# adaLN block with local dilated attention and GEGLU: first products interleaved over two PSUM banks, first norm scaled chunk by chunk, 14 warm-up products, another written-out order

## The chip, the core and the metric

The kernel runs on one core of one Trainium2 chip. The metric is device time in microseconds (us) of one execution; the median of several runs is compared. A profile is taken of one execution more, and all lines of a trace in this document come from such a profile.

## The reference

One transformer block on x of 2048 rows by 512 columns (bf16), with shift, scale and gate vectors (sa, ca, ga, sb, cb, gb) from `silu(c) @ w_mod`.

```
h   = layernorm(x) * (1 + ca) + sa
qkv = h @ wqkv                      # 32 heads of 16
logits[s, w] = q[s] . k[s - 2w] / 4   for w = 0..7, masked where s - 2w < 0
o   = sum_w softmax(logits)[s, w] * v[s - 2w]
x   = x + ga * (o @ wo)
h   = layernorm(x) * (1 + cb) + sb
x   = x + gb * ((gelu(h @ w_gate) * (h @ w_up)) @ w_down)   # inner width 1792
```

## The kernel before

**Tiling.** The 2048 rows are four groups of 512 rows (`sg` 0 to 3); a group is four chunks of 128 rows (`c4`). The 512 columns are four pieces of 128 (`dt`), the inner width 1792 is 14 pieces (`ft`).

**Stages of a group**, with the names that the profile and this text use:

- First norm `LN1.sg`. VectorE (DVE) takes mean and variance of a chunk (`st`, lines 410 and 411, 0.8 us a chunk), or ScalarE (ACT) does it for the chunks that the table `ACT_CH` names (`sa` line 388, `nm` line 394, `sq` line 399). DVE adds epsilon (`vd` line 436 for its own chunks, `va` line 441 for ACT's), GpSimd (POOL) raises to -1/2 (`rs`, line 447), and DVE scales the chunks (`x`, line 424).
- Transposes on TensorE (PE), or by DMA for some groups; then scale and shift by the modulation vectors give the pieces `h0` to `h3` of hT (ACT line 498; in group 0 ACT line 516 and DVE line 514, half a group at a time).
- Products `qp.sg.blk.j`: 12 for a group, each 4 matmuls over `dt` into one PSUM bank (line 565; in group 0 the first two are done in halves of 256 rows, `qph`, line 547). ACT copies each out (lines 579, 581, 585).
- Logits: DVE multiplies q by shifted k (`pq`, line 631, 2.3 us, four a group), PE sums over the head (`lp`, line 645), DVE and ACT do the softmax, DVE multiplies by v (`pv`), PE sums (`o`, line 796), or in group 3 DVE does (`os` line 758, `ot2` line 763, `ob` line 770).
- Output projection `x1p` (line 817), added to x by DVE (`x1`, line 826); second norm `LN2.sg`; products `g` and `u` (line 845), ACT's gelu `gl` (line 878) and copy `ub` (line 885), DVE's product `hh` (line 896); then `y` (line 857, in the last chunk line 868), DVE's sum `ot` (line 903), and the store.

**PSUM.** The pool `mm` has 4 banks, shared by qkv, g, u, y, the vectors of modulation (`mp`) and the warm-up products. The buffers of `gl` and `ub` are three each: a fourth `gl` waits for `hh` of the third before it.

**Order.** Nothing is scheduled at run time. Each stage of each group is a generator ("thread") of `Op`s; the list `ORDER` says which thread issues its next op. It fixes the sequence on each engine's queue, DMA issues on SP and ACT included. The numbers in an `Op` (its cost, `lat`) are not used when the kernel is built; `after` is only asserted.

**At the start**, PE runs 20 products on a zeroed tile (`warmup`, line 213, spread between the first real ones), then `mp1`, `mp0` (line 296: columns of the modulation vectors, from `wm1`, `wm0`), the transposes `th0`, `th1` of group 0's two halves (line 483), and `qph`. The op `pre` (line 330) is a four-element Exp on ACT, ahead of which the exp table is loaded. POOL builds small constants (`consts`, `M2`).

Sequences of the queues where the text needs them (from `ORDER`, thread by thread):

```
PE, start        8 warm, scp, 8 warm, mp1, 2 warm, mp0, th0, th1, 2 warm, qph ...
PE, group 1      LN1.1.t0, mp2, t1, mp3, lp.0.0-2, lp.0, qp.1.0.0, qp.1.1.0, qp.1.2.0-3, LN1.2.t0 ...
ACT, start       s4, scT, pre, scB, mod1, mod0, h0.0, h1.0, h0.1, LN1.1.sa3 ...
DVE, start       st0, st1, vd0, st2, st3, vd2, x0, x1, x2, x3, h2.0, h3.0, h1.1, h2.1, h3.1, LN1.1.st0 ...
DVE, group 3     ... pv.3.3, hh.2.0, hh.2.1, os.3.1, ot2, ob, os.3.2, ot2, ot.1.1, ot.1.2, ob, os.3.3, ot2, ob, hh.2.2, hh.2.3, ot.1.3 ...
SP               ... x2, wo0, wo1, wm2, wm3, wo2, wo3, x3, vst.0, gst2, wm4, V4.0.0 ...
```

Of the kernel before, what the change touches and what calls it, by code (L numbers as in the profile page):

```python
# [8 lines left out]
ACT = mybir.ActivationFunctionType  # L9
ALU = mybir.AluOpType  # L10
AX = mybir.AxisListType
F32 = mybir.dt.float32
# [93 lines left out]
def kernel(  # L106
# [13 lines left out]
    nc = tc.nc  # L120
    P = 128
# [95 lines left out]
    def loads():  # L217
# [43 lines left out]
        def act_q():  # L261
            yield Op("ACT", 0.45, ldc, fire="c", lat=0.0, dma=True)
            yield Op("ACT", 0.46, ldx(0, 2, 4, nc.scalar), fire="x0.2", lat=1.45, dma=True)

        def sp_q():
            yield Op("SP", 0.47, ldx(0, 0, 2), fire="x0.0", lat=1.0)
            yield Op("SP", 0.47, ldwm(1), take=[SL["h2"]], fire="wm1", lat=3.2)
            yield Op("SP", 0.5, ldwm(0), take=[SL["h2"]], fire="wm0", lat=1.4)
            yield Op("SP", 0.55, ldq(0), fire="wqkv0", lat=mb(0.5))
            yield Op("SP", 0.55, ldx(1), fire="x1", lat=mb(0.5))  # L270
            yield Op("SP", 0.55, ldq(1), fire="wqkv1", lat=mb(0.5))
            yield Op("SP", 0.55, ldq(2), fire="wqkv2", lat=mb(0.5))
            yield Op("SP", 0.55, ldx(2), fire="x2", lat=mb(0.5))
            for i in range(4):
                yield Op("SP", 0.45, ld(woP[H * i:H * i + H, :, :], wo_v[i]), fire=f"wo{i}", lat=0.42)
            yield Op("SP", 0.55, ldx(3), fire="x3", lat=mb(0.5))
# [97 lines left out]
    ACT_CH = {"LN1.1": (3, 4), "LN1.2": (2, 4), "LN1.3": (0, 4), "LN2.0": (0, 2), "LN2.1": (0, 4), "LN2.2": (0, 2), "LN2.3": (0, 2)}  # L374
# [28 lines left out]
    def norm(key, src, ready, ev, parts=((0, 4),)):  # L403
        aa, ab = ACT_CH.get(ev, (0, 0))
        dv = [c4 for c4 in range(CPS) if not aa <= c4 < ab]
        for c4 in dv:
            def f(c4=c4):
                k = norm_tiles(ev)
                st = stat.tile([P, 6], F32, name="st")
                nc.vector.bn_stats(out=st[:], in_=src()[:, c4, :])  # L410
                nc.vector.bn_aggr(out=k["mv"][:, c4, :], in_=st[:])
            yield Op("DVE", 0.815, f, after=ready(c4), fire=f"{ev}.st{c4}")
            for a, b in parts[:-1]:
                if c4 == b - 1:
                    yield from rst(ev, a, b, [c4 for c4 in dv if a <= c4 < b])
        a, b = parts[-1]
        yield from rst(ev, a, b, [c4 for c4 in dv if a <= c4 < b])
        for c4 in range(CPS):
            def f(c4=c4):
                k = norm_tiles(ev)  # L420
                if c4 == 0:
# [4 lines left out]
            yield Op("DVE", 0.325, f, after=[f"{ev}.rs{max(a for a, b in parts if a <= c4)}"],  # L426
                     take=[SL["xn"]] if c4 == 0 else [], fire=f"{ev}.x{c4}")
# [112 lines left out]
    def qkv_halves():  # L540
        for half in range(2):
            def f(half=half):
                for j in range(2):
                    if half == 0:
                        B["qkvps", 0, 0, j] = T("mm", [P, SG], F32, "qkv_ps")
                    for dt in range(DT):
                        nc.tensor.matmul(B["qkvps", 0, 0, j][:, half * 256:half * 256 + 256],
                                         lhsT=wqkv[0][:, dt, j::4], rhs=B["hT", 0][:, 2 * half:2 * half + 2, dt, :],
                                         start=(dt == 0), stop=(dt == DT - 1))
            yield Op("PE", 0.87, f, after=[f"LN1.0.h{d}.{half}" for d in range(DT)] + ["wqkv0"],  # L550
                     take=[SL["mm"]] * 2 + [SL["q"]] if half == 0 else [], fire=f"qph.{half}")
        for j in range(2):
            pl.done[f"qp.0.0.{j}"] = pl.done["qph.1"]

    def qkv(sg):
        if sg == 0:
            yield from qkv_halves()
        for n, (blk, j) in enumerate(QKV if sg else QKV0):
            if (sg, blk) == (0, 0) and j < 2:
                continue  # L560
# [192 lines left out]
    def osum(sg):  # L753
        for i in range(4):
# [4 lines left out]
            yield Op("DVE", 2.19, f, after=[f"pv.{sg}.{i}"], take=[SL["prod"]], give=[SL["prod"]], fire=f"os.{sg}.{i}")  # L759
# [4 lines left out]
            yield Op("DVE", 1.12, f, fire=f"ot2.{sg}.{i}")  # L764
# [72 lines left out]
    def ffn_mm(sg):  # L837
        h2 = [f"LN2.{sg}.h3"]
        for ft in range(FT):
# [95 lines left out]
    pl.spawn(warmup(13, 20))  # L935
# [3 lines left out]
    for sg in range(NSG):  # L939
        for n, g in (("sa1", lambda q: norm_act(lambda: B["x", q], lambda c4: [f"x{q}"], f"LN1.{q}")),  # L940
# [37 lines left out]
```

## Time and profile before

| what | value |
|---|---|
| median of 3 runs | 238.0 us (237.67 to 238.57) |
| the profiled execution | 237.54 us |
| its span, first to last instruction | 235.8 us |
| busy share: PE, DVE, ACT, POOL | 97%, 77%, 66%, 5% |
| granted TensorE clock, mean | 1.000 |
| chain that ended last, by engine | PE 75%, DVE 14%, ACT 8% |
| PE LDWEIGHTS busy | 108.9 us (46%) |
| DMA, mean | 121 GB/s |

The span is the time between the first and the last instruction; 1.74 us of the profiled execution lie outside. "Busy" of PE counts matmuls from start to modelled end, and since they are pipelined (a 128x512 product has a row of 379 ns, while neighbours start 216 ns apart), PE is read here from starts, not from busy time.

### The profile page before, as it was taken

Reading aid. Unit: us, or ns where it says so; the run is one execution under the profiler, and the core shown is the slowest. Engines: PE = TensorE matmul, PEld = TensorE weight load, DVE = VectorE, ACT = ScalarE, POOL = GpSimd, SP = SyncE. Lnnn points to the kernel's source line nnn. Section 1 sums busy time; section 2 is a strip of 40 time slices with the busy share of each in tenths; the row PEclk is TensorE's granted clock in tenths of the full one; section 3 lists DMA queues with packets and bytes.
Section 4 is the critical chain, followed back from the end, with each engine's and each line's share of the span. In section 5 each row is a group of like instructions: output and inputs, shape, how many; then the busy total and the mean of one; then the engine's idle time right before and its main releaser. Section 6 shows DMA issues by size and latency. Waiting matters only on the chain.

```text
span 235.8 us, 3655 instructions
## 1 busy us (share of the span) xinstructions
PE 229.8 (97%) x1371; PEld 108.9 (46%) x1371; DVE 182.2 (77%) x244; ACT 154.7 (66%) x301; POOL 12.5 (5%) x37
## 2 busy tenths in 40 slices
PE   7999899999999999999999999999999999999995
PEld 2656364544544444444444444444344444444444
DVE  3889999999999999999999899999728521222222
ACT  4589999986996649957687878422567343667400
POOL 1620101000100000100000100000000100000000
PEclk9999999999999999999999999999999999999999
DMA  6998797999965859634104014001230141000011
GB/s 216 350 306 233 219 196 176 192 347 326 195 172 162 288 120 198 155 70 120 59 0 100 1 37 98 25 0 67 62 95 3 31 102 44 3 0 0 0 44 44
DMA packets 36792, 28.64 MB, mean 121 GB/s; under 512 B 15784, under 2 KB 35368, under 8 KB 36776
## 3 DMA queue, kind: packets, MB, share of 16 engines
q1 hardware_dynamic: 36496, 28.17, 46.4%
q10 hardware_dynamic: 280, 0.26, 0.3%
q8 instruction: 10, 0.16, 0.3%
q14 instruction: 6, 0.05, 0.1%
HBM read 21.08 MB, written 5.24 MB: 112 GB/s over the span
## 4 chain that ended last, share of the span: by engine, by line
PE 75%; DVE 14%; ACT 8%; issue 1%; DVEq 0%; ACTq 0%
PE u_ps L845 16%; PE g_ps L845 15%; PE y_ps L857 14%; PE qkv_ps L565 12%; PE x_ps L817 6%; DVE os L758 4%; DVE pv L738 4%; PE warm_ps L213 3%; PE o_ps L796 2%; PE LTp L645 2%; DVE hht L896 2%; ACT vT L585 2%; ACT gl L399 2%; DVE os L763 2%; ACT gl L388 2%
## 5 line engine op out<-in xcount | busy, mean ns | idle before, releaser
L845 PE MATMUL u_ps<-h,Wu 128*128 128x512 bf16 x224 | 57.5, 379 | 0.5 <-ACT gl L878 0.5
L845 PE MATMUL g_ps<-h,Wg 128*128 128x512 bf16 x224 | 57.5, 379 | 0.0
L878 ACT ACTIVATE gl<-g_ps 128x512 bf16<-128x512 f32 x56 | 33.6, 600 | 20.6 <-PE g_ps L845 16.7
L857 PE MATMUL y_ps<-Wd,hht 128*128 128x512 bf16 x210 | 46.3, 379 | 0.0
L885 ACT CAST ub<-u_ps 128x512 bf16<-128x512 f32 x56 | 32.9, 587 | 20.3 <-PE u_ps L845 20.2
L565 PE MATMUL qkv_ps<-hT,wqkv 128*128 128x512 bf16 x184 | 41.8, 380 | 0.6 <-ACT qT L579 0.6
L896 DVE TENSOR_TENSOR hht<-gl,ub 128x512 bf16<-128x512 bf16 x56 | 22.1, 418 | 23.5 <-ACT ub L885 23.4
L631 DVE TENSOR_TENSOR pq<-qT,kT 128x4096 bf16<-128x4096 bf16 x16 | 36.0, 2284 | 0.7 <-ACT kT L581 0.7
L845 PEld LDWEIGHTS <-Wu 128*128 128x128 bf16 x224 | 21.6, 98 | 27.9 <-issue 2.5
L845 PEld LDWEIGHTS <-Wg 128*128 128x128 bf16 x224 | 21.8, 98 | 26.8 <-issue 0.8
L857 PEld LDWEIGHTS <-hht 128*128 128x128 bf16 x210 | 20.6, 98 | 24.8
L565 PEld LDWEIGHTS <-wqkv 128*128 128x128 bf16 x184 | 20.3, 114 | 20.3 <-issue 3.3
L748 DVE TENSOR_TENSOR pv<-PT,V 128x4096 bf16<-128x4096 bf16 x12 | 26.7, 2282 | 0.0
L903 DVE TENSOR_TENSOR ot<-y_ps,x 128x512 bf16<-128x512 f32 x15 | 10.1, 686 | 14.7 <-PE y_ps L857 14.7
L447 POOL TENSOR_TENSOR rstd<-rstd,neghalf 128x4 f32<-128x4 f32 (+1 forms) x9 | 8.6, 961 | 170.7 <-DVE rstd L441 164.8
L498 ACT ACTIVATE h<-h,modT,scl 128x512 bf16<-128x512 bf16 x12 | 8.8, 802 | 9.7 <-DMA h<-xn 9.7
L817 PE MATMUL x_ps<-woP,oT 128*128 128x512 bf16 x64 | 15.1, 379 | 0.0
L826 DVE TENSOR_TENSOR x<-x_ps,x 128x512 bf16<-128x512 f32 x16 | 10.7, 682 | 3.1 <-PE x_ps L817 3.0
L410 DVE BATCH_NORM_STATS2 st<-x 128x6 f32<-128x512 bf16 x15 | 10.1, 676 | 3.0 <-DMA x<-in_A_x_dram 3.0
L399 ACT ACTIVATE gl<-x,sums 128x512 bf16<-128x512 bf16 x17 | 12.3, 730 | 0.2
L388 ACT ACTIVATE gl<-x 128x512 bf16<-128x512 bf16 x17 | 10.7, 643 | 2.2 <-DVE x L826 2.0
L581 ACT CAST kT<-qkv_ps 128x512 bf16<-128x512 f32 x16 | 9.8, 612 | 0.9 <-PE qkv_ps L565 0.8
(82 smaller groups left out, 202.5 us busy)
## 6 DMA issues: line engine op xcount, KB each, us to landing
V<-vscr SPq DMA_DIRECT2D x8, 520.0 KB, 11.3
wm<-in_w_mod_dram SPq DMA_DIRECT2D x6, 512.0 KB, 4.7
vscr<-vT SPq DMA_DIRECT2D x4, 512.0 KB, 4.9
out_dram<-ot SPq DMA_DIRECT2D x15, 128.0 KB, 1.8
Wg<-in_B_w_gate_dram SPq DMA_DIRECT2D x1, 1792.0 KB, 9.1
Wu<-in_B_w_up_dram SPq DMA_DIRECT2D x1, 1792.0 KB, 12.7
wqkv<-in_A_wqkv_dram SPq DMA_DIRECT2D x3, 512.0 KB, 7.7
x<-in_A_x_dram SPq DMA_DIRECT2D x3, 512.0 KB, 8.5
```

What stands on the lines that cost most here:

```text
L388: nc.scalar.activation(out=gpool.tile([P, D], BF16, name="gl")[:], in_=src()[:, c4, :], func=ACT.Copy, accum_out=k["s"][:, 0, c4:c4 + 1])
L399: nc.scalar.activation(out=gpool.tile([P, D], BF16, name="gl")[:], in_=src()[:, c4, :], func=ACT.Square, bias=k["s"][:, 1, c4:c4 + 1], acc ...
L565: nc.tensor.matmul(ps[:], lhsT=wqkv[blk][:, dt, j::4], rhs=B["hT", sg][:, :, dt, :], start=(dt == 0), stop=(dt == DT - 1))
L631: nc.vector.tensor_tensor(out=pq[:], in0=_ap(B["qT", sg][:, j, :], [[0, W], [1, SG]]), in1=_ap(kT[:, j, sg * SG + 2:sg * SG + 2 + SG], [[2 ...
L748: nc.vector.tensor_tensor(out=t[:], in0=_ap(B["PT", sg][:, 0, :], [[SG, 2], [0, 4], [1, SG]]), in1=_ap(v[:, 0, j, :], [[8, 2], [4 * (SG + ...
L817: nc.tensor.matmul(ps[:], lhsT=B["oT", sg][:, j, c4 * P:(c4 + 1) * P], rhs=woP[:, j, :], start=(j == 0), stop=(j == 3))
L826: nc.vector.tensor_tensor(out=x[:, c4, :], in0=B["x1ps", sg, c4][:], in1=x[:, c4, :], op=ALU.add)
L845: nc.tensor.matmul(ps[:], lhsT=Wt[:, dt, ft * P:(ft + 1) * P], rhs=B["h2T", sg][:, :, dt, :], start=(dt == 0), stop=(dt == DT - 1))
L857: nc.tensor.matmul(ps[:], lhsT=B["hh", sg, ft][:, c4 * P:(c4 + 1) * P], rhs=B["Wd", ft // 4][:, ft % 4, :], start=(ft == 0), stop=(ft == F ...
L878: nc.scalar.activation(out=gl[:], in_=B["g", sg, ft][:], func=ACT.Gelu_apprx_tanh)
L885: nc.scalar.copy(out=ub[:], in_=B["u", sg, ft][:])
L896: nc.vector.tensor_tensor(out=hh[:], in0=B["gl", sg, ft][:], in1=B["ub", sg, ft][:], op=ALU.mult)
```

## The change

1. `warmup(12, 14)`: 14 warm-up products in place of 20.
2. `ACT_CH` gets `LN1.0: (3, 4)`: statistics of chunk 3 of the very first norm go from DVE to ACT; DVE gets one small `va2` for it. The DVE part of `norm` is rewritten: chunks of a part are scaled as soon as the statistics of the next part are issued, so `x0`, `x1` stand ahead of `vd2`. Only `LN1.0` has two parts; for all other norms the sequence is the same.
3. `qkv_halves`: the two products of a half of group 0 go piece by piece over two banks (`qph.half.n`, pieces 2, 0, 3, 1, then 1, 0, 2, 3) where each product ran its four pieces before.
4. `qkv_pair` (new): in groups 1 to 3 the products (q, j=0) and (k, j=0) go piece by piece over two banks (`qpp.sg.dt`). `ffn_mm`: the first `g` and first `u` likewise (`gu.sg.dt`).
5. `ORDER` is another list. The number of matmuls other than warm-up products is the same.

```diff
-    ACT_CH = {"LN1.1": (3, 4), ...
+    ACT_CH = {"LN1.0": (3, 4), "LN1.1": (3, 4), ...
...
+        done = []
+        for a, b in parts:
+            for c4 in dv:
+                if a <= c4 < b:
+                    yield stats(c4)
+            for c4 in done:
+                yield scaled(c4)
+            yield from rst(ev, a, b, [c4 for c4 in dv if a <= c4 < b])
+            done = range(a, b)
+        for c4 in done:
+            yield scaled(c4)
...
     def qkv_halves():
-        for half in range(2):
-            def f(half=half):
-                for j in range(2):
...
+        for half, order in ((0, (2, 0, 3, 1)), (1, (1, 0, 2, 3))):
+            for n, dt in enumerate(order):
+                def f(half=half, n=n, dt=dt):
+                    for j in range(2):
...
+    def qkv_pair(sg):
+        for dt in range(DT):
+            def f(dt=dt):
+                for blk in range(2):
+                    if dt == 0:
+                        B["qkvps", sg, blk, 0] = T("mm", [P, SG], F32, "qkv_ps")
+                    nc.tensor.matmul(B["qkvps", sg, blk, 0][:], lhsT=wqkv[blk][:, dt, 0::4], rhs=B["hT", sg][:, :, dt, :],
+                                     start=(dt == 0), stop=(dt == DT - 1))
...
     def ffn_mm(sg):
-        for ft in range(FT):
+        for dt in range(DT):
+            def f(dt=dt):
+                for nm, Wt in (("g", Wg), ("u", Wu)):
+                    if dt == 0:
+                        B[nm, sg, 0] = T("mm", [P, SG], F32, nm + "_ps")
+                    nc.tensor.matmul(B[nm, sg, 0][:], lhsT=Wt[:, dt, 0:P], rhs=B["h2T", sg][:, :, dt, :],
+                                     start=(dt == 0), stop=(dt == DT - 1))
...
+        for ft in range(1, FT):
...
-    pl.spawn(warmup(13, 20))
+    pl.spawn(warmup(12, 14))
```

What `ORDER` makes of the queues, at the places named above:

```
PE, start        8 warm, scp, 6 warm, th0, mp1, mp0, th1, qph ...
PE, group 1      LN1.1.t0, t1, lp.0.0, lp.0.1, mp2, qpp.1.0-3, lp.0.2, lp.0, mp3, qp.1.2.0-3, qp.1.0.1, qp.1.1.1, qp.1.0.2, LN1.2.t0 ...
PE, group 0 att. ... o.0.0, qpp.3.0, qpp.3.1, o.0.1, lp.1.2, o.0.2, qpp.3.2, qpp.3.3, qp.2.0.2, o.0.3, qp.2.1.2, x1p.0.0, x1p.0.1, lp.1 ...
ACT, start       s4, scT, LN1.0.sa3, nm, sq3, pre, mod1, mod0, h0.0, h1.0, h0.1, LN1.1.sa3 ... (scB later)
DVE, start       st0, st1, vd0, st2, x0, x1, vd2, va2, x2, x3, h2.0, h3.0, h1.1, h2.1, h3.1, LN1.1.st0 ...
DVE, group 3     ... pv.3.3, os.3.1, ot2, ob, ot.1.1, hh.2.0, hh.2.1, ot.1.2, os.3.2, ot.1.3, ot2, ob, os.3.3, hh.2.2, ot2, hh.2.3, ob, hh.2.4 ...
SP               ... x2, wo0, wo1, wo2, wo3, x3, wm2, wm3, vst.0, wm4, gst2, V4.0.0 ...
POOL             ident, consts, LN1.0.rs0, rs2, M2 ... (before: ident, rs0, rs2, consts, M2)
```

In group 2 the output projection `x1p.2.2` stands ahead of `u.1.6` (before: behind it), and `x1p.3.0` behind `u.2.11`.

More of the change, by code (lines that the diff above doesn't have):

```diff
@@ L262, in act_q @@
             yield Op("ACT", 0.45, ldc, fire="c", lat=0.0, dma=True)
-            yield Op("ACT", 0.46, ldx(0, 2, 4, nc.scalar), fire="x0.2", lat=1.45, dma=True)
+            yield Op("ACT", 0.46, ldx(0, 2, 4, nc.scalar), fire="x0.2", lat=2.3, dma=True)
         def sp_q():
             yield Op("SP", 0.47, ldx(0, 0, 2), fire="x0.0", lat=1.0)
-            yield Op("SP", 0.47, ldwm(1), take=[SL["h2"]], fire="wm1", lat=3.2)
+            yield Op("SP", 0.47, ldwm(1), take=[SL["h2"]], fire="wm1", lat=2.45)
             yield Op("SP", 0.5, ldwm(0), take=[SL["h2"]], fire="wm0", lat=1.4)
@@ L372, in woscale @@
         yield Op("DVE", 1.14, wos, after=["ga"] + [f"wo{i}" for i in range(4)], fire="woS")
-    ACT_CH = {"LN1.1": (3, 4), "LN1.2": (2, 4), "LN1.3": (0, 4), "LN2.0": (0, 2), "LN2.1": (0, 4), "LN2.2": (0, 2), "LN2.3": (0, 2)}
+    ACT_CH = {"LN1.0": (3, 4), "LN1.1": (3, 4), "LN1.2": (2, 4), "LN1.3": (0, 4), "LN2.0": (0, 2), "LN2.1": (0, 4), "LN2.2": (0, 2), "LN2.3": (0, 2)}
     NS = {}
@@ L405, in norm, with stats, f @@
         dv = [c4 for c4 in range(CPS) if not aa <= c4 < ab]
-        for c4 in dv:
-            def f(c4=c4):
+        def stats(c4):
+            def f():
                 k = norm_tiles(ev)
@@ L411, in f, with scaled @@
                 nc.vector.bn_aggr(out=k["mv"][:, c4, :], in_=st[:])
[L412 to L419, printed above, removed]
+            return Op("DVE", 0.815, f, after=ready(c4), fire=f"{ev}.st{c4}")
+        def scaled(c4):
+            def f():
                 k = norm_tiles(ev)
@@ L425, in f @@
                                         scalar2=k["rstd"][:, c4:c4 + 1], op0=o, op1=ALU.mult)
-            yield Op("DVE", 0.325, f, after=[f"{ev}.rs{max(a for a, b in parts if a <= c4)}"],
-                     take=[SL["xn"]] if c4 == 0 else [], fire=f"{ev}.x{c4}")
+            return Op("DVE", 0.325, f, after=[f"{ev}.rs{max(a for a, b in parts if a <= c4)}"],
+                      take=[SL["xn"]] if c4 == 0 else [], fire=f"{ev}.x{c4}")
+        done = []
[9 more added lines that the diff above has]
+            yield scaled(c4)
     def rst(ev, a, b, dv):
@@ L540, in qkv_halves @@
     def qkv_halves():
-        for half in range(2):
-            def f(half=half):
-                for j in range(2):
-                    if half == 0:
-                        B["qkvps", 0, 0, j] = T("mm", [P, SG], F32, "qkv_ps")
-                    for dt in range(DT):
+        for half, order in ((0, (2, 0, 3, 1)), (1, (1, 0, 2, 3))):
+            for n, dt in enumerate(order):
+                def f(half=half, n=n, dt=dt):
+                    for j in range(2):
+                        if half == 0 and n == 0:
+                            B["qkvps", 0, 0, j] = T("mm", [P, SG], F32, "qkv_ps")
                         nc.tensor.matmul(B["qkvps", 0, 0, j][:, half * 256:half * 256 + 256],
                                          lhsT=wqkv[0][:, dt, j::4], rhs=B["hT", 0][:, 2 * half:2 * half + 2, dt, :],
-                                         start=(dt == 0), stop=(dt == DT - 1))
-            yield Op("PE", 0.87, f, after=[f"LN1.0.h{d}.{half}" for d in range(DT)] + ["wqkv0"],
-                     take=[SL["mm"]] * 2 + [SL["q"]] if half == 0 else [], fire=f"qph.{half}")
+                                         start=(n == 0), stop=(n == DT - 1))
+                yield Op("PE", 0.2175, f, after=[f"LN1.0.h{dt}.{half}", "wqkv0"],
+                         take=[SL["mm"]] * 2 + [SL["q"]] if half == n == 0 else [], fire=f"qph.{half}.{n}")
         for j in range(2):
-            pl.done[f"qp.0.0.{j}"] = pl.done["qph.1"]
+            pl.done[f"qp.0.0.{j}"] = pl.done["qph.1.3"]
+    def qkv_pair(sg):
[6 more added lines that the diff above has]
+                                     start=(dt == 0), stop=(dt == DT - 1))
+            yield Op("PE", 0.437, f, after=[f"LN1.{sg}.h{dt}", "wqkv0", "wqkv1"],
+                     take=[SL["mm"]] * 2 + [SL["q"]] if dt == 0 else [], fire=f"qpp.{sg}.{dt}")
+        for blk in range(2):
+            pl.done[f"qp.{sg}.{blk}.0"] = pl.done[f"qpp.{sg}.3"]
     def qkv(sg):
@@ L557, in qkv @@
             yield from qkv_halves()
+        else:
+            yield from qkv_pair(sg)
         for n, (blk, j) in enumerate(QKV if sg else QKV0):
-            if (sg, blk) == (0, 0) and j < 2:
+            if (sg == 0 and blk == 0 and j < 2) or (sg and n < 2):
                 continue
@@ L758, in f @@
                 nc.vector.tensor_tensor(out=t[:], in0=a[:, :, 0:4, :], in1=a[:, :, 4:8, :], op=ALU.add)
-            yield Op("DVE", 2.19, f, after=[f"pv.{sg}.{i}"], take=[SL["prod"]], give=[SL["prod"]], fire=f"os.{sg}.{i}")
+            yield Op("DVE", 2.31, f, after=[f"pv.{sg}.{i}"], take=[SL["prod"]], give=[SL["prod"]], fire=f"os.{sg}.{i}")
             def f(i=i):
@@ L763, in f @@
                 nc.vector.tensor_tensor(out=t[:, :, 0:2, :], in0=t[:, :, 0:2, :], in1=t[:, :, 2:4, :], op=ALU.add)
-            yield Op("DVE", 1.12, f, fire=f"ot2.{sg}.{i}")
+            yield Op("DVE", 1.25, f, fire=f"ot2.{sg}.{i}")
             def f(i=i):
@@ L838, in ffn_mm @@
         h2 = [f"LN2.{sg}.h3"]
-        for ft in range(FT):
+        for dt in range(DT):
[5 more added lines that the diff above has]
+                                     start=(dt == 0), stop=(dt == DT - 1))
+            yield Op("PE", 0.437, f, after=[f"LN2.{sg}.h{dt}", "Wg", "Wu"], take=[SL["mm"]] * 2 if dt == 0 else [],
+                     fire=f"gu.{sg}.{dt}")
+        for nm in "gu":
+            pl.done[f"{nm}.{sg}.0"] = pl.done[f"gu.{sg}.3"]
+        for ft in range(1, FT):
             for nm, Wt, wk in (("g", Wg, "Wg"), ("u", Wu, "Wu")):
@@ L939 @@
     for sg in range(NSG):
-        for n, g in (("sa1", lambda q: norm_act(lambda: B["x", q], lambda c4: [f"x{q}"], f"LN1.{q}")),
+        for n, g in (("sa1", lambda q: norm_act(lambda: B["x", q], lambda c4: [f"x{q}"] if q else [f"x0.{c4 // 2 * 2}"], f"LN1.{q}")),
                      ("sa2", lambda q: norm_act(lambda: B["x", q], lambda c4: [f"x1.{q}.{c4}"], f"LN2.{q}")), ("ln1", ln1), ("t1", lambda q: transp(("xn1", q), ("hT", q), "hT", f"LN1.{q}") if q else transp0(("xn1", 0), "LN1.0")), ("h1", lambda q: ln1_ev(q) if q else ln1_ev0(False)), ("qkv", qkv),
```

67 rows, old and new, of the table ORDER are left out of this document.

## The prediction

> **What bounds the kernel now.** First the table of busy time by stretch (columns: stretch, its length, then busy us and instructions of PE, PE's weight loads, DVE, ACT, POOL).
>
> ```profile
> 14.90:54.40 39.50, 38.10 (x317) 19.75 (x315) 39.29 (x39) 35.99 (x78) 2.40 (x3) 1.00 0.91 232
> 54.40:132.00 77.60, 77.60 (x483) 35.10 (x482) 76.33 (x87) 59.49 (x115) 2.05 (x2) 1.00 0.60 144
> 132.00:167.00 35.00, 35.00 (x164) 15.88 (x163) 34.53 (x42) 17.85 (x31) 1.05 (x1) 1.00 0.15 38
> ```
>
> Two engines are full at once up to 167 us: PE, and DVE with 39.29 of 39.50, 76.33 of 77.60 and 34.53 of 35.00 us. After 167 DVE is free (22.58 of 68.80 us) and PE alone sets the end. Then PE's own row in order of time, which names each stall in brackets:
>
> ```profile
> 25.10 0.61 PE L645 MATMUL LTp<-pq,Mph 128*32 128x512 bf16 x8 [0.77 <-DVE pq L631]
> ...
> 29.74 1.89 PE L565 MATMUL qkv_ps<-hT,wqkv 128*128 128x512 bf16 x8 [0.45 <-ACT qT L579]
> ...
> 35.70 2.75 PE L565 MATMUL qkv_ps<-hT,wqkv 128*128 128x512 bf16 x12 [0.18 <-ACT qT L579]
> ...
> 168.00 1.02 PE L845 MATMUL u_ps<-h,Wu 128*128 128x512 bf16 x4 [0.52 <-ACT gl L878]
> ```
>
> By starts (neighbours 0.216 us apart) these stalls are 1.09, 0.61, 0.34 and 0.68 us: three before 36 us, one at 168, nothing between. The chain of waits says what stands behind the last:
>
> ```profile
> 130.36 1.74 PE x_ps L817 x8
> 132.12 0.69 DVE x L826
> ...
> 166.84 0.43 DVE hht L896
> 167.31 0.04 issue
> 167.35 0.60 ACT gl L878
> 167.96 0.04 issue
> 168.00 1.02 PE u_ps L845 x4
> ```
>
> From 132 to 167 the chain runs on DVE: `hh.2.2` at 166.84 comes behind group 3's sums, a gelu waits for its buffer, PE for the gelu's bank. So DVE decides how far PE may run ahead until 167, and PE's stalls decide afterwards.
>
> **The start.** These rows set it (start, duration):
>
> ```profile
> 5.18 1.28 ACT L330 ACT_TABLE_LOAD   x1
> ...
> 7.87 0.73 DVE L424 TENSOR_SCALAR xn<-x,mv,rstd 128x512 bf16<-128x512 bf16 x2
> ...
> 8.87 0.73 DVE L424 TENSOR_SCALAR xn<-x,mv,rstd 128x512 bf16<-128x512 bf16 x2 [0.27 <-POOL rstd L447]
> ...
> 14.86 2.29 DVE L631 TENSOR_TENSOR pq<-qT,kT 128x4096 bf16<-128x4096 bf16 x1 [0.75 <-ACT kT L581]
> ```
>
> DVE. Chunk 2's statistics start at 6.05, when x lands, and end at 6.96. Then `x0`, `x1` run 7.00 to 7.73, 0.87 earlier. The second half is not earlier. ACT begins chunk 3 at 6.05 too; the same five instructions of LN1.1 take from 10.88 to 12.68, 1.80 us, so they end at 7.86. `va2` follows at 7.92, POOL 0.30 later for 0.80 us (its row at 8.04), so `x2`, `x3` run 9.05 to 9.78; they ended at 9.60. Loss 0.18.
>
> ACT. `pre` with its table load now follows `sq3`: 7.87 to 9.38, then `mod1`, `mod0` to 9.55, and the pieces `h` from 9.70, against 9.52. [...]
>
> PE. 14 warm-up products end near 7.4, `th0` runs at 7.8, `mp1` and `mp0` (0.4 each) until 9.05, `th1` waits for `x3` and ends at 10.25. `qph` needs `h2.0` (DVE 9.70 to 10.11) and begins at 10.30 instead of 10.49. Its pieces take 0.22 and the eight `h` arrive every 0.32 on DVE and 0.46 on ACT, in just the order in which they are used; the last, `h3.1`, is there at 11.55, its piece starts at 11.83. End 12.05 against 12.24. The six products taken out (2 by 0.43, 4 by 0.22, 1.7 us) thus bring 0.2: behind them the norm is late.
>
> And that 0.2 goes no further: DVE's full stretch begins with `pq.0.0`, which waits for ACT's copy of k, and ACT, 0.18 late, reaches that at 14.19 (before 14.17). `pq.0.0` at 14.87 instead of 14.86: nothing.
>
> **14.9 to 54 us.** DVE's ops up to `pq.1.3` are the same set, without a gap; so `pq.1.3` still ends at 54.34. PE may now stall less: `qpp.1` begins when `h0` is there. I add ACT's rows: it reaches `LN1.1.h0` at 21.3 instead of 22.80 (`sq3` and the gate copy, 0.86, go behind; PE's products come 0.2 to 0.3 earlier there and an idle 0.28 ahead of 16.76 is used), so `qpp.1` runs about 22.8 to 24.6 where `qp.1.0.0` began at 25.64. On PE's queue `mp2` stands ahead of it and needs `wm2`, which SP now issues behind wo2, wo3, x3. Up to wm2's end the queue has then carried the same bytes as before up to wo3's, and wo3 landed at 23.09: some 0.6 us of waiting, at most. By the sums PE stands 0.5 to 1.1 us ahead at 41 us. It then meets DVE: `o.0.3` needs `pv.0.3` (ends 51.00) and `lp.1` needs `pq.1.3`: 54.40 instead of 54.63. **Kept: 0.23.** The two extra splits between four-column and full products (0.2 us each by the starts at 47.37 to 47.68 and 48.78 to 49.09) lie ahead of this wait and cost nothing.
>
> **54 to 167.** PE had no stall and has the same products, with as many splits: the lead stays 0.23. I checked the waits that the new order makes: `lp.2.1` (pq.2.1 ends 70.03, PE there at 70.27), `gu.0` to `gu.3` (a piece takes 0.43, ACT delivers every 0.67 to 0.71, but between two and six other ops stand ahead of them; the closest, gu.1, begins 0.8 us behind its `h0` and may lack 0.05 at the last piece). `x1p.2.2` moved ahead of `u.1.6` ends DVE's gaps at 131.26 and 132.12 (0.44 and 0.17).
>
> **167.** `hh.2.2` is moved ahead of `ot2` and `ob` (1.26 and 0.61) and behind one `ot` more (0.60): 1.27 earlier, with the gaps up to 1.9. Also `ot.1.3`, which held a fourth bank, is done 7 us earlier. **The stall of 0.68 goes.** Next late is `hh.2.4`, no earlier than before (done at 168.5) and needed 0.5 us after that.
>
> **After 167.** PE's work is the same. LN2.3's four scalings follow each other without two `hh` between (0.67 earlier), and `gu.3.0` comes 3.0 us earlier behind y.2's sixth half: x1p.3.3 to `h0` took 11.5 us, less 0.67, against 11.66 in the new order. No stall, 0.8 us of cover.
>
> **Banks alternating.** 24 products of `qpp`, 32 of `gu` and 16 of `qph` change bank at each product. Before, g and u change it at every fourth, with the same 0.216 us between starts: I take nothing. The dearest change in the rows, into or out of four-column products, costs 0.1; 72 by 0.1 is 7.2 us, the far end. [...]
>
> **Sum.** 0.23 + 0.68 = 0.9 us: span 234.9, the profiled execution 237.54 - 0.9 = 236.6. The median of the runs was 238.0, 0.46 above it, and I forecast on that scale: **237.1**. More than 0.5% (1.2 us, about what a measurement of this kernel tells from no change) would need an earlier `pq.0.0`.
>
> **Rivals.**
>
> - **The clock opens late (slower).** Warm-up products started every 0.427 us until 7.0 and every 0.216 from then, so full speed came 6.0 us after the first product. The new ones end at 7.4; `th0`, `mp`, `th1` fill only half of the time to 10.3. Were the array slow then until 6.0 us of products have run again, PE would lose 3.0 us, of which ACT's lateness hides 0.3: 237.1 + 2.7 = 239.8. It decides from the point where `qph` starts 0.2 us apart instead of 0.11. For it: six fillers stood exactly there. Against: 1.1 idle us at 24 did not lower the clock. Chance 0.15. [...]
> - **`wm2` lands late.** Past 23.2 us `mp2` holds `qpp.1`, ACT's copy, `LN1.3.sq3` and with it `va0` on DVE (needed at 35.2); each us later costs one. At 24.6: 238.5. Chance 0.12.
> - **The table load stops ACT's queue longer than its row**, at most by its own length once more: `h` and `pq.0.0` 1.28 later, 238.4. Against it: 0.02 and 0.01 us beside the row. Chance 0.05.
> - **Alternating banks cost** something: from 237.1 up to 244.3. Chance 0.03.
> - **More comes through at the start** (ACT's copy of k at 13.9, as PE allows): 0.3 more, 236.8 or lower. Chance 0.1.
> - The forecast: 0.55, 236.6 to 237.7 by the runs' own scatter.
>
> The range 236.4 to 239.0 leaves out the late clock's upper part and the dear banks. Below 236.8 lie the last rival and a quarter of the forecast: faster 0.22; above 239.2 the late clock mostly: slower 0.16; within 0.5%: 0.62.
>
> **What would show it.** Right: `xn` pairs near 7.0 and 9.05, `qph` near 10.3 with 0.11 between starts, `pq.0.0` at 14.9, `lp.1` at 54.4, no PE wait for `gl` near 167, 216 ns between products of `qpp` and `gu`. Wrong: starts of 0.2 us in `qph`, PE or ACT waiting at `mp2`, a new gap on DVE before 54 us, which moves the end by its own length.

## The result and the profile after

The changed kernel is a little **slower**: a median of 239.2 us (237.59 to 240.6, 17 runs) against 238.0 us (237.56 to 239.22, 17 runs) for the kernel before, measured side by side. The ratio is 1.005, with a 95% interval of 1.0027 to 1.0073. The forecast was 237.1, "slower" had a chance of 0.16.

The profiled execution took 240.6 us, its span 238.6, with a mean granted clock of 0.986. It is one of the two slowest of the 17, and the runs differ in just that: 5 of 17 have a clock of 1.000 (span 235.6 to 237.2, median 236.0), 10 have 0.993 (237.1 to 238.2, median 237.5), 2 have 0.986 (238.6). The kernel before is at 0.998 or more in 95 of the 99 runs that the experiments below added. So the first line to read is the clock in slices, on the page of the changed kernel (each digit is a fortieth of the span, 6 us):

```profile
PEclk9779999999999999999999999999999999999999
```

Slices two and three, 6 to 18 us, are not at full speed. In the kernel before all forty are a 9. (The slow start itself does not show in the digits: before, the warm-up products came 0.427 us apart until 7.0, in slices that print 9.) PE's row in order of time (start, duration, then what ran; in brackets the idle time and who ended it) shows where. First two rows of the kernel before, then the changed kernel:

```profile
9.03 1.19 PE L483 MATMUL hTp<-ident,xn 128*128 128x128 bf16 x16
...
10.49 1.91 PE L547 MATMUL qkv_ps<-hT,wqkv 128*128 128x256 bf16 x16
```

```profile
4.89 1.59 PE L214 MATMUL warm_ps<-gB 128*128 128x512 bf16 x6
8.50 1.25 PE L492 MATMUL hTp<-ident,xn 128*128 128x128 bf16 x8 [2.02 <-DVE xn L421]
9.54 1.04 PE L297 MATMUL modT_ps<-scT,wm 128*128 128x1 bf16 x32
10.51 1.25 PE L492 MATMUL hTp<-ident,xn 128*128 128x128 bf16 x8
11.55 3.62 PE L556 MATMUL qkv_ps<-hT,wqkv 128*128 128x256 bf16 x16
14.97 1.25 PE L589 MATMUL qkv_ps<-hT,wqkv 128*128 128x512 bf16 x4
```

The warm-up products end at 6.5, then PE rests for 2.0 us. The transposes behind the rest start 0.107 us apart (in the kernel before 0.056), and the 16 products of `qph` take 3.4 us by their starts, 0.213 apart (forecast 0.11). Full speed had come at 5.2 us, when warm-up products went from 0.427 to 0.216 us apart; it was gone at 8.6 and came back at 15.4 (granted clock 1.00 for 3.4 us, then 0.50 for 6.8). The first `pq` starts at 17.81 instead of 14.86: 2.95 us are lost ahead of it.

Not all of the 2.95 us is the clock. DVE's row of chunk 2's statistics says when the second half of x landed, at 7.23 here and at 6.05 in the kernel before; and the run f1 (below), where it landed at 7.19 and the clock stayed at full speed, starts its first `pq` at 15.87. The rows, of the changed kernel and of f1:

```profile
7.23 0.69 DVE L411 BATCH_NORM_STATS2 st<-x 128x6 f32<-128x512 bf16 x1 [1.66 <-DMA x<-in_A_x_dram]
```

```profile
15.87 2.29 DVE L656 TENSOR_TENSOR pq<-qT,kT 128x4096 bf16<-128x4096 bf16 x1 [0.77 <-ACT kT L606]
```

By f1 some 1.0 us of the 2.95 belongs to x, and 1.9 to the clock.

The next loss is in the chain of waits, here from 99.86 us on (start, duration, what). Before, the chain from 94 to 112 us ran on PE alone:

```profile
99.86 1.80 DVE Wd L367 x3
...
102.83 2.33 POOL rstd L456
...
105.19 1.40 DVE xn L421 x4
...
106.64 4.39 DMA h<-xn
...
111.77 2.22 ACT h L507 x3
```

POOL's `rstd` of `LN2.1`, four elements a partition, takes 2.3 us where it took 1.04 before:

```profile
98.26 1.04 POOL L447 TENSOR_TENSOR rstd<-rstd,neghalf 128x4 f32<-128x4 f32 x1 [36.17 <-DVE rstd L441]
```

DVE waits 0.90 us for it, the transposes by DMA and ACT's pieces of h come later, and PE, which begins `gu.1` when its first piece is there, stalls:

```profile
111.99 0.38 PE L868 MATMUL g_ps<-h,Wg 128*128 128x512 bf16 x1
112.21 0.38 PE L868 MATMUL u_ps<-h,Wu 128*128 128x512 bf16 x1
112.62 0.38 PE L868 MATMUL g_ps<-h,Wg 128*128 128x512 bf16 x1
...
113.33 0.38 PE L868 MATMUL g_ps<-h,Wg 128*128 128x512 bf16 x1
...
114.03 0.38 PE L868 MATMUL g_ps<-h,Wg 128*128 128x512 bf16 x1
```

The pairs start 0.63, 0.71 and 0.70 apart; without a stall it is 0.43. The sum of what is too much is 0.75 us.

The rest went nearly as forecast. `lp.1` starts at 57.40, 2.77 later than before, so PE gained 0.18 on DVE's late start (forecast 0.23). The stall of 0.68 near 167 is gone. Alternating g and u start 0.216 apart wherever their piece is there. The account of the two profiled spans, with clock and x in the first term: 2.95 - 0.18 + 0.75 - 0.68 = 2.84, and 238.6 - 235.8 = 2.8.

### The profile page after: what moved, and what is told of

The parts are those of the page before. It is cut to its first block, busy times and chain, and to the rows that moved or that the text cites. A ratio compares the mean times of both kernels' runs of the same rounds, so it can differ in the third digit from the quotient of the medians.

```text
span 238.6 us, 3636 instructions
## 1 busy us (share of the span) xinstructions
PE 230.9 (97%) x1355; PEld 108.9 (46%) x1365; DVE 181.1 (76%) x243; ACT 156.4 (66%) x306; POOL 13.6 (6%) x37
## 4 chain that ended last, share of the span: by engine, by line
PE 68%; DVE 11%; DMA 7%; ACT 7%; issue 3%; POOL 1%; SPq 0%; ACTq 0%; POOLq 0%
PE g_ps L880 16%; PE u_ps L880 16%; PE y_ps L892 15%; PE qkv_ps L589 7%; PE x_ps L841 4%; DMA V<-vscr 3%; DVE pv L772 3%; DMA x<-in_A_x_dram 2%; DVE pq L655 2%; DMA h<-xn 2%; ACT vT L609 2%; PE LTp L669 2%; DVE Wd L367 2%; PE o_ps L820 1%; ACT gl L389 1%
## 5 line engine op out<-in xcount | busy, mean ns | idle before, releaser
L880 PE MATMUL g_ps<-h,Wg 128*128 128x512 bf16 x208 | 53.4, 379 | 0.0
L880 PE MATMUL u_ps<-h,Wu 128*128 128x512 bf16 x208 | 53.4, 379 | 0.0
L589 PE MATMUL qkv_ps<-hT,wqkv 128*128 128x512 bf16 x160 | 36.8, 381 | 0.3 <-ACT qT L603 0.3
L880 PEld LDWEIGHTS <-Wu 128*128 128x128 bf16 x208 | 20.1, 98 | 25.1 <-issue 1.3
L880 PEld LDWEIGHTS <-Wg 128*128 128x128 bf16 x208 | 20.1, 98 | 25.1 <-issue 1.3
L589 PEld LDWEIGHTS <-wqkv 128*128 128x128 bf16 x160 | 17.8, 114 | 16.3 <-issue 1.5
L456 POOL TENSOR_TENSOR rstd<-rstd,neghalf 128x4 f32<-128x4 f32 (+1 forms) x9 | 9.8, 1093 | 173.9 <-DVE rstd L450 170.8
L389 ACT ACTIVATE gl<-x 128x512 bf16<-128x512 bf16 x18 | 11.3, 636 | 6.8 <-DVE x L850 3.7
L400 ACT ACTIVATE gl<-x,sums 128x512 bf16<-128x512 bf16 x18 | 13.1, 738 | 0.2
L603 ACT CAST qT<-qkv_ps 128x512 bf16<-128x512 f32 x16 | 9.7, 612 | 2.6 <-PE qkv_ps L589 1.4
```

Source lines behind the costliest of these rows:

```text
L389: nc.scalar.activation(out=gpool.tile([P, D], BF16, name="gl")[:], in_=src()[:, c4, :], func=ACT.Copy, accum_out=k["s"][:, 0, c4:c4 + 1])
L400: nc.scalar.activation(out=gpool.tile([P, D], BF16, name="gl")[:], in_=src()[:, c4, :], func=ACT.Square, bias=k["s"][:, 1, c4:c4 + 1], acc ...
L589: nc.tensor.matmul(ps[:], lhsT=wqkv[blk][:, dt, j::4], rhs=B["hT", sg][:, :, dt, :], start=(dt == 0), stop=(dt == DT - 1))
L880: nc.tensor.matmul(ps[:], lhsT=Wt[:, dt, ft * P:(ft + 1) * P], rhs=B["h2T", sg][:, :, dt, :], start=(dt == 0), stop=(dt == DT - 1))
```

## The experiments

All were timed beside the kernel before, whose median was 237.8 to 237.9. "Closed" below counts the runs with a granted clock of 0.993 or less. Two theories stood at the start. **Theory:** with fewer warm-up products, and PE at rest for 2.0 us behind them, the clock closes, and `gu.1`'s stall takes away the forecast gain. **Rival:** the clock is beside the point; the norm part or the late arrival of x makes the loss.

| kernel | warm-up products | runs, closed | median us | median span at full clock |
|---|---|---|---|---|
| before (beside all the others) | 20 | 99, 4 | 237.8 to 237.9 | 235.9 to 236.1 |
| changed | 14 | 17, 12 | 239.2 | 236.0 |
| e1 changed, six more | 20 | 12, 1 | 237.9 | 235.9 |
| e2 before, six fewer | 14 | 12, 6 | 237.8 | 235.6 |
| e3 `va0` earlier | 14 | 12, 6 | 238.5 | 235.8 |
| e5 norm as before | 14 | 12, 9 | 239.4 | 236.2 |
| f1 logits ahead of `gu.1` | 20 | 12, 3 | 238.0 | 235.6 |
| f2 `pq.3.1` behind `va0` | 20 | 12, 0 | 237.5 | 235.45 |
| f3 no interleaving | 20 | 6, 1 | 241.5 | 239.4 |
| f4 `hh.2.2` late | 20 | 12, 1 | 238.2 | 236.2 |
| g1 f1 and f2 together | 22 | 12, 1 | 237.6 | 235.4 |
| g2 six more, other place | 20 | 12, 1 | 237.9 | 235.9 |
| g3 x by SP | 22 | 12, 1 | 238.4 | 236.4 |
| g4 a memset at `LN2.1` | 20 | 12, 1 | 237.1 | 235.0 |

**e1: the six products back.**

```diff
-    pl.spawn(warmup(12, 14))      # PE: 8 warm, scp, 6 warm, th0, mp1, mp0, th1, qph
+    pl.spawn(warmup(12, 20))      # PE: 8 warm, scp, 12 warm, th0, mp1, mp0, th1, qph
```

> The changed kernel with six more warm-up products behind its fourteen (20, as before). Theory (the gap between the warm-up products and the transposes lets the TensorE clock close): the mean granted clock is 1.000 in nearly all runs where the changed kernel had 0.993 or 0.986 in 12 of 17; a closed stretch cost about 1.7 us, so the median goes from 239.2 to the changed kernel's full-clock runs, 237.6 to 238.4. Rival (the loss is the later arrival of x and the norm part, 1.2 us, and the stall at gu.1, 0.75 us): clock mix and median as in the changed kernel, 239.2, or 0.2 more.

The clock closed in 1 of 12 runs instead of 12 of 17, and the median fell from 239.2 to 237.9. PE's row:

```profile
4.89 2.99 PE L215 MATMUL warm_ps<-gB 128*128 128x512 bf16 x12
7.71 0.64 PE L493 MATMUL hTp<-ident,xn 128*128 128x128 bf16 x8
...
9.47 0.89 PE L493 MATMUL hTp<-ident,xn 128*128 128x128 bf16 x8 [0.34 <-DVE xn L422]
10.20 1.91 PE L557 MATMUL qkv_ps<-hT,wqkv 128*128 128x256 bf16 x16
```

`qph` takes 1.9 us again, begins at 10.20 (forecast 10.30), and `pq.0.0` starts at 14.87 (forecast 14.87). So it went as the theory expected. But the span is 235.7, not the forecast 234.9: `gu.1` still stalls for 0.75.

**e2: the kernel before with 14.** Two of the eight products behind `scp` and the two pairs further on are out; nothing else of the change is in.

```diff
-    pl.spawn(warmup(13, 20))      # 8 warm, scp, 8 warm, mp1, 2 warm, mp0, th0, th1, 2 warm, qph
+    pl.spawn(warmup(13, 14))      # 8 warm, scp, 6 warm, mp1, mp0, th0, th1, qph
```

> The kernel before with 14 warm-up products (two of the eight behind scp, and the two pairs among mp0, th1 and qph, taken out), nothing else changed. Theory: the warm-up products alone do it, so the clock falls to 0.993 in a good part of the runs, each by some 1.7 us, and the median goes from 238.0 to 239 or 239.7. Rival (the norm part or the interleaving is what leaves PE idle): clock 1.000, median 237.8 to 238.2.

Half of the runs closed, at 237.1 instead of 235.6 us of span: 1.5 us for a clock of 0.993. The median did not come as expected: it is 237.8, the middle between two heaps at 237.3 and 238.8, and taken alone it would speak for the rival. The clocks of the runs show the effect. So taking out the warm-up products does it alone, and with x at its usual time (6.19 in the profile). Its profile is one of the closed runs: full speed at 6.3, transposes 0.107 apart from 9.8 on, full speed back at 13.1.

**e5: the norm part undone**, with 14 warm-up products.

```diff
-    ACT_CH = {"LN1.0": (3, 4), "LN1.1": (3, 4), ...
+    ACT_CH = {"LN1.1": (3, 4), ...
...                                # norm() as in the kernel before; pre directly behind scT
```

> The changed kernel with the first norm as before (chunk 3 on DVE, both pairs scaled after all statistics, the exp table loaded early), still 14 warm-up products. Theory: the gap behind the warm-up products stays (the first transposes come no earlier), so most runs still have a clock of 0.993 or less: median 239.0 to 240. Rival (the norm part makes the loss): clock 1.000 and 237.5 to 238.2.

9 of 12 runs closed, so the norm part is not what closes the clock and that half of the rival falls. (Its other half, a late x, costs 1.0 us in f1's profile, at full clock.) At full clock its span is 236.2 (three runs) against 236.0 for the changed kernel (five, 235.6 to 237.2): no more than the scatter, so what the norm part is worth, forecast at 0.2 us, is not shown.

**e3: `LN2.1.va0` earlier.**

```diff
- DVE: ... WdS4, hh.0.10, WdS5, va0, WdS6, hh.0.11, hh.0.12, hh.0.13, x0 ...
+ DVE: ... WdS4, va0, hh.0.10, WdS5, WdS6, hh.0.11, hh.0.12, hh.0.13, x0 ...
```

> The changed kernel with LN2.1.va0 two DVE instructions earlier (directly behind WdS4, where ACT's sums are there since 101.3 us). Theory: POOL's rstd, 2.32 us there, is then done before DVE needs it, DVE's gap of 0.90 us and the stalls in gu.1 (0.75 us) go, and the time of runs with an equal clock falls by 0.7 us: clock 0.993 runs from 239.5 to 238.8, median from 239.2 to 238.5. Rival (DVE decides again behind it, so PE's 0.75 us are waited for elsewhere): no change, 239.2. The mix of clocks stays as in the changed kernel.

A miss, though the median of 238.5 is the expected one: that is luck, since 6 of 12 runs closed and not 12 of 17, and the span at full clock fell by 0.2 (235.8), not 0.7. DVE's gap stayed at 0.90 us and the stalls in `gu.1` too, because `rstd` now took 3.26 us. In both orders it ended 0.86 us behind the end of `hh.0.13`, the last product ahead of `x0`, wherever it had started. So the length of POOL's row goes by where DVE's products end, at least in these two orders; f2 and g4 change what stands there.

**f2: `pq.3.1` behind `va0`**, on e1.

```diff
- DVE: hh.0.9, pq.3.1, WdS2, WdS3, WdS4, hh.0.10, WdS5, va0, WdS6, hh.0.11 ...
+ DVE: hh.0.9, WdS2, WdS3, WdS4, hh.0.10, WdS5, WdS6, va0, pq.3.1, hh.0.11 ...
```

> The kernel of e1 with the DVE order at LN2.1.va0 near that of the kernel before: WdS6 ahead of va0, and pq.3.1 (2.28 us) directly behind it. Theory: POOL's rstd takes 2.32 us in e1 and 3.26 in e3 because it ends only 0.86 us after the last short bf16 product of DVE (WdS, hh); beside the one long pq it took 1.05 in the kernel before, so 1.05 here, xn some 0.5 us earlier, and the stalls in gu.1 shrink from 0.75 to about 0.25: span 235.2. Rival (POOL is slow for another reason, such as its long rest): again over 2 us, xn not earlier, span 235.7 or more.

The time came near to what was expected (span 235.45 against 235.2, the stall down to 0.18), but not by the reason given: `rstd` took 2.91 us, ending 0.87 behind the end of `pq.3.1`. So beside a long `pq` it can take as long, and the part of the theory that spoke of short products is wrong. x came earlier only because `va0` did.

**g4: a memset in the string of products**, on e1.

```diff
                 B["hh", sg, ft] = hh
+                if (sg, ft) == (0, 11):
+                    nc.vector.memset(stat.tile([P, 6], F32, name="st")[:], 0.0)
                 nc.vector.tensor_tensor(out=hh[:], in0=B["gl", sg, ft][:], in1=B["ub", sg, ft][:], op=ALU.mult)
```

> The kernel of e1 with one small DVE memset (128x6, no input) between WdS6 and hh.0.11, that is inside the string of bf16 products during which POOL's rstd did not end. [...] Rival (POOL waits for DVE to come to rest): rstd again 2.4 us, span 235.7 to 235.9.

First POOL's row in the changed kernel, then in g4, and g4's rows of DVE:

```profile
102.83 2.32 POOL L456 TENSOR_TENSOR rstd<-rstd,neghalf 128x4 f32<-128x4 f32 x1 [37.85 <-DVE rstd L450]
```

```profile
99.82 1.31 POOL L457 TENSOR_TENSOR rstd<-rstd,neghalf 128x4 f32<-128x4 f32 x1 [37.85 <-DVE rstd L451]
```

```profile
99.59 0.69 DVE L368 TENSOR_TENSOR Wd<-Wd,gB 128x1024 bf16<-128x1024 bf16 x1
100.20 0.42 DVE L934 TENSOR_TENSOR hht<-gl,ub 128x512 bf16<-128x512 bf16 x1
100.22 0.06 DVE L933 MEMSET st<- 128x6 f32 x1
100.53 0.75 DVE L934 TENSOR_TENSOR hht<-gl,ub 128x512 bf16<-128x512 bf16 x2
101.20 1.38 DVE L422 TENSOR_SCALAR xn<-x,sums,rstd 128x512 bf16<-128x512 bf16 x4
```

With 0.06 us of DVE work that has no input in the string, `rstd` took 1.31 us and not the rival's 2.4: it ended at 101.13, 0.85 behind the memset and behind `WdS6`, which both end at 100.28 (in e1, without the memset, it took 2.32). The gap ahead of `xn` is gone, and `gu.1` starts its eight products 0.216 apart. The span of the profiled run is 234.9, the number of the forecast's sum, and the median is 237.14, 0.9972 of the kernel before (0.9949 to 0.9996). It is the lowest median of all; f2 has the same ratio (0.9972, 0.9946 to 0.9997), so the two can't be told apart against the kernel before.

**f1: logits ahead of `gu.1`**, on e1: the other cure, on PE's side.

```diff
- PE: ... y.0.2.1, gu.1.0, gu.1.1, gu.1.2, gu.1.3, lp.3.0, lp.3.1, lp.3.2 ...
+ PE: ... y.0.2.1, lp.3.0, lp.3.1, gu.1.0, gu.1.1, gu.1.2, gu.1.3, lp.3.2 ...
```

> The kernel of e1 (20 warm-up products) with lp.3.0 and lp.3.1 ahead of gu.1.0 instead of behind gu.1.3. Theory: PE's stalls in gu.1 (0.75 us in the profile of e1: pairs 0.63, 0.71 and 0.71 apart where 0.43 is free) come from pieces that ACT delivers every 0.71 us, the first at 108.9; 0.86 us of logits ahead of them cover that, so the stalls go, the span goes from 235.7 to 235.0 and the median from 237.9 to 237.2. Rival (DVE decides behind it): no change, 235.7 to 235.9.

The stalls are gone (0.216 apart), but only 0.3 us of span at full clock, not 0.7. In its profiled run the second half of x landed at 7.19 instead of 6.2 and `pq.0.0` came 1.0 later at full clock; how much of the missing 0.4 that accounts for in the other runs is open.

**g1: f1 and f2 together**, and two more warm-up products between `mp0` and `th1`.

> The kernel of e1 with both edits at gu.1 (lp.3.0 and lp.3.1 ahead of it; WdS6 ahead of LN2.1.va0 and pq.3.1 behind it) and two more warm-up products between mp0 and th1 (22 in all). Theory: no stall in gu.1, full clock in all runs, span 235.0 to 235.4, median 237.0 to 237.4, the fastest of all. Rival (each edit moves the same wait, DVE decides behind it): as f2, 235.45 and 237.46.

No stall in `gu.1`, yet 235.4 at full clock, as f2 alone: the second cure adds nothing that the runs show. Its time can't be told from the kernel before (0.9986, 0.9962 to 1.001).

**f3: interleaving undone** in groups 1 to 3 and for g and u, on e1 (`qkv_pair` and the `gu` loop out, whole products in the places of their third and fourth step).

> The kernel of e1 with the interleaving over two banks undone in groups 1 to 3 (qpp) and in the second half (gu): each product runs its four pieces into one bank, in the places of the third and fourth step; qph stays. Theory (the alternation costs nothing by itself and lets PE begin before the last piece): gu.1 has to wait for the last piece, at 111.06 instead of beginning at 109.06, with the later order shift a loss of 1.0 to 1.5 us there, little elsewhere: span 236.5 to 237.5. Rival (alternating banks cost something): up to 0.1 us for each of 56 products, so the span falls below 235.7.

3.5 us longer than e1 at full clock, more than expected and the opposite of the rival. PE waits for ACT's pieces of h again, here in `g.1.0` (0.20 + 0.33 + 0.33 us by the brackets):

```profile
111.89 0.38 PE L868 MATMUL g_ps<-h,Wg 128*128 128x512 bf16 x1
112.47 0.38 PE L868 MATMUL g_ps<-h,Wg 128*128 128x512 bf16 x1 [0.20 <-ACT h L508]
113.18 0.38 PE L868 MATMUL g_ps<-h,Wg 128*128 128x512 bf16 x1 [0.33 <-ACT h L508]
113.88 0.38 PE L868 MATMUL g_ps<-h,Wg 128*128 128x512 bf16 x1 [0.33 <-ACT h L508]
```

By starts that is 1.34 us, with 0.37 at 69, 0.49 at 197, 0.75 around 40 and 1.27 around 24; 0.73 at 36 is a wait for a bank behind them. Those ahead of 54 us are partly hidden by DVE. The interleaving is what makes the new order possible, and it has no price of its own that a row shows.

**f4: `hh.2.2` late again**, on e1.

```diff
- DVE: ... os.3.3, hh.2.2, ot2, hh.2.3, ob, hh.2.4 ...
+ DVE: ... os.3.3, ot2, ob, hh.2.2, hh.2.3, hh.2.4 ...
```

> The kernel of e1 with hh.2.2 and hh.2.3 behind ot2.3.3 and ob.3.3 again, as in the kernel before (1.87 us of DVE work moved ahead of them). Theory (the stall of 0.68 us near 167 was ended by hh.2.2's place): a wait for gl of 0.5 to 0.8 us comes back on PE there and the span goes to 236.2 to 236.5. Rival (the stall went by another part, ot.1.3 or x1p.2.2): no stall, 235.7 to 235.9.

A stall came back at 168.82, but of 0.31 us, and the median span rose by 0.3. So the place of `hh.2.2` is worth about half of the 0.68. The other half is not accounted for: f4 keeps other parts of the new order (`ot.1.3` early, `x1p.2.2`), and they were not tried one by one.

**g2: six products in another place** (20 in all, the six between `mp0` and `th1`).

> The changed kernel with 20 warm-up products again, but the six extra ones between mp0 and th1 instead of directly behind the others: the rest of PE between the warm-up products and th0 stays. [...] Rival (only the number of products counts): 0 or 1 of 12. Rival (any rest of 1 to 2 us closes it): half of the runs or more.

1 of 12 closed, as many as in e1; the rival that only the number of products counts had named 0 or 1, and the one that any rest of 1 to 2 us closes the clock had named half of the runs or more. The profiles of other kernels differ in one more thing. Lay the 3.41 us for which full speed held in the changed kernel's profile (its clock record: 5.17 to 8.58) behind the moment at which full speed came in each, and add up 0.42 ns for each column that a product fed (512 take 0.216 us). Products then filled 33% of it in the changed kernel and, by the spacing of the warm-up products, some 30% in e2 and e3, where the clock closed; 70% in the kernel before and, by the spacing, some 80% in e1, where it stayed open. Whether this share decides, or the number of products, no run shows.

**g3: the second half of x by SP**, on g1.

```diff
-            yield Op("ACT", 0.46, ldx(0, 2, 4, nc.scalar), fire="x0.2", lat=2.3, dma=True)
+            yield Op("SP", 0.47, ldx(0, 2, 4), fire="x0.2", lat=2.3)      # behind x0.0, ahead of wm1
```

> The kernel of g1 with the load of chunks 2 and 3 of x issued by SP directly behind x0.0 instead of by ACT. In the profiles so far that load landed anywhere from 6.05 to 7.2 us, with the first pq from 14.9 to 15.9 at full clock. Theory (it competes with wm1 and wm0, which SP issues at the same time): it lands near 5.0 each time and spans scatter less: 234.8 to 235.3. Rival (the landing scatters for another reason, or mp1 now waits for wm1): no gain, or up to 0.5 us more than g1.

The load of x stands first now, but `mp0` waits 0.75 us for its weights, DVE 0.88 for `mod0`, and a product of group 0 0.20 for `wqkv`: 1 us longer than g1 (236.4 against 235.4). Putting one load first moved the wait to others.

## Why the prediction was wrong, point by point

- **The start: the step that failed.** "14 warm-up products end near 7.4, `th0` runs at 7.8 ... begins at 10.30 ... Its pieces take 0.22": nearly true in e1 with 20 products, where `th0` and `qph` came at 7.71 and 10.20. In the changed kernel the clock closes first. It opened at 5.2 in the profiled run, 4.0 us after the first product; in the kernel before that was 6.0, in the others between 2.8 (g3) and 6.0. So the moment of opening, which the forecast took from one profile, is not fixed, and the six products taken out had filled the time behind it: of the next 3.4 us products filled 33% in the changed kernel's profile and some 80% in e1's (of the kernels made from the changed one with 20 or 22 products, 10 of 102 runs closed still). The forecast said that taking them out would "bring 0.2: behind them the norm is late": about right as work on PE, wrong as to what they are for. In its place stand 1.5 us for each run at a clock of 0.993 (changed kernel at full clock 236.0 us of span, at 0.993 237.5), and 12 of 17 runs were at 0.993 or 0.986. The other 1.1 us between the forecast's 234.9 and the 236.0 is `gu.1`'s 0.75 and a rest that no single row names.
- **The rival was named, at 0.15.** "The clock opens late" had the sign, the place (starts of 0.2 us in `qph`) and nearly the time (239.8; measured 239.2). The nearness is partly luck, for what happened was another thing: not a late opening but a closing behind it, at a price of 1.5 us for a clock of 0.993 (e2, and the changed kernel's 236.0 to 237.5) and 2.6 for 0.986 (236.0 to 238.6); and `gu.1`, which stalls at full clock as well (e1), added 0.75. The argument against it, "1.1 idle us at 24 did not lower the clock", was no argument: in e3's profile the clock closed with rests of 0.32 and 0.34 us in brackets, so the length of one rest says little. Fewer warm-up products close it (e1, e2); by what, no run shows. The clock also differs between runs of one kernel (5 of 17 at 1.000 for the changed one), so one profile at 1.000 says nothing of the others. The four kernels with 14 products closed in 33 of 53 runs; a chance of 0.15 was far too low. The range left out "the late clock's upper part": no row shows a lower one, and the changed kernel's ten runs at 0.993 took 239.05 to 240.19.
- **x lands when it lands.** The forecast took 6.05 us from one profile. In the others with the same load it was 5.8 to 6.7, and twice 7.2, the changed kernel's among them. At full clock 7.19 cost 1.0 us (f1, `pq.0.0` at 15.87). ACT issues that load at 1.4 us in both kernels, so it is taken here for scatter and not for a part of the change; with two profiles of the old order (6.05 and 6.19) this is not shown.
- **14.9 to 54, "Kept: 0.23".** Right: 0.18 in the changed kernel, 0.17 in e1. `mp2` did not wait for `wm2`, and the table load held up nothing beyond its row (Exp 0.02 us behind it; in the kernel before the load began 0.02 behind the end of the copy ahead of it, and the Exp 0.01 behind the load).
- **54 to 167, "gu.1 ... may lack 0.05".** Wrong in size: 0.75. The chain from `va0` to `h0` was taken with POOL's 1.04 us from the old neighbours. POOL ended 0.86 us behind a product of DVE, in the changed kernel behind the fourth that ran beside it.
- **167, "the stall of 0.68 goes".** Right, with about half of it from the step that the forecast named (f4).
- **Banks alternating: nothing.** Right: 0.216 between starts, and f3.
- **The sum.** Span 234.9 was forecast, 234.9 is g4's, the change at full clock (1.000) and with `rstd` at 1.31 us. So the two gains of the sum hold, and what it lacked were these two losses. e1, with the clock alone, is 235.9, no better than before. A smaller term was missed: 1.74 us lie outside of the span in the kernel before (1.7 to 1.8 in its later runs and in e2), 2.0 in every kernel made from the changed one. That 0.2 us is why g4 gains 0.8 on the median where its span gains 1.0. No trace shows what it is, and it stays open.

## What to carry to other kernels

Products that compute nothing may be holding the clock: with six of them out it closed in 33 of 53 runs here, with them in 10 of 102, and a run at 0.993 was 1.5 us longer. So take them out alone first, as e2 does, in enough runs to see how often the clock closes. Read the granted clock of all the runs, not of the profiled one, and split the times by it before comparing medians: e2's median showed nothing, its clocks all. And take the duration of a small POOL operation together with what DVE runs beside it, since the same four elements took from 1.04 to 3.26 us here.

## What was not expected of the hardware

- The clock closed while PE had work: in the changed kernel's profile after 3.4 us at full speed of which products filled 33%, with a rest of 2.0 us; in e3 and e2 (some 30%) with shorter rests only, 0.32 and 0.34 us in e3 and 0.43 in e2.
- POOL's `rstd` of four elements took from 1.04 to 3.26 us, by the order of DVE's products beside it. In all profiles `rstd` of `LN2.1` ended 0.85 to 0.87 us behind the end of a DVE instruction: 1.04 us in all in the kernel before (behind `hh.0.10`), 2.32 in the changed one (behind the fourth product), 3.26 in e3 (behind the sixth), 1.31 in g4 (behind the memset). In the changed kernel three products that started after POOL's row (103.19 and later, against 102.83) ended before it. Why it ended behind the first product in one order and behind the last in another isn't shown, but the rows say in which. Of the 28 rows of `rstd` in `LN2.1` and `LN2.2` of the fourteen profiles, the eight in which a `WdS` product stood in the string beside POOL ended behind the string's last product (2.32 to 3.26 us), and the 19 without one ended 0.86 to 0.87 behind the first product, whatever followed it; the last is g4, with `WdS6` and the memset. No run took `WdS` alone out of the string, so that it is the cause is not shown.
